# Attention scores as three fp32r products, with operand parts made by GpSimd, on one Trainium2 core

## The chip, the cores and the metric

The kernel runs as one program on one core of one Trainium2 chip. The metric is the device time of one execution in microseconds (us), told as a median of runs; lower is better.

## The reference

Two stages, all in float32. Attention with a bias that depends on position (batch 4, 8 heads, 576 positions, head size 64), then a feed-forward layer (2304 tokens, 512 to 2048 to 512) with a softplus between its two products.

```python
scores = q @ k.T / sqrt(D)                      # per batch and head, 576 x 576
x    = log1p(|i - j|) / log1p(max(i, 1))
bias = relu(x * w1 + b1) @ w2                   # one value per head, i, j
scores = scores + bias
attn = exp(scores - rowmax); attn /= rowsum + 1e-9
a    = attn @ v                                 # to (2304, 512)
out  = softplus(a @ moe_w_in) @ moe_w_out
```

## The kernel before

**The stages.** Up to about 62 us of the profiled span the bias is made, 16 rows at a time (36 steps), and written to DRAM (`e_d`). Then come the attention rounds. One round is one unit `n` (0 to 15: a pair of heads of one batch element). The rounds 2 to 14 are the steady ones; each takes 12.35 us. After round 16 comes the feed-forward layer, to the end at 673.7 us: per step twelve matmuls into `h` (L784) and twelve into `y` (L842), each already a sum of three fp32r products of a rounded part and the rest (`w_fin` at L751 and `x_prep` at L769 make the two parts with ScalarE and VectorE).

**One round.** A round is written by hand as a list of tokens (`ROUND`, L45). All engines take their instructions in the order of that list, each engine only its own, and no engine overtakes within itself. The loop at L969 hands each token to `emit` (L578):

- `S7/1` computes score tile 7 of the next unit, n+1, into PSUM bank 1 (`u_s`, L320, matmuls L347). The nine tiles of a unit are 128 rows by 576 columns; tile t is 128 queries of one head against all keys, tile 4 holds the last 64 queries of both heads. The head size of 64 fills half of TensorE's rows, so a tile is made as two halves of 288 columns, one on rows 0 to 63 and one on rows 64 to 127. These are plain fp32 matmuls, and the trace shows each of them as two instructions. There are four banks: 0, 1, 2 (the trace calls it `t`) and `o`.
- `A7` (VectorE, L365) adds the bias tile, takes the row minimum and puts the result to SBUF; `X7` (ScalarE, L383) is the exponential with its row sum.
- `L0` to `L4` (GpSimd, L400, `tail`) copy the last 64 columns of two tiles together.
- `T10/2` transposes three blocks of unit n into a bank (`turn`, L405), and `V10/a` or `V10/d` copies them to SBUF on ScalarE (a, L316) or VectorE (d, L318).
- `P0` to `P4` (L470) multiply by v; `P3` and `P4` of a unit stand in the next round. `O` (VectorE, L490) multiplies the output by the reciprocal row sums `rb`, and `Y` (L496 to L499) stores it with four DMAs to `x_d`.
- `I` (L508, L509) makes the reciprocals, `R` transposes them, `C` copies them to SBUF on ScalarE (L524) and stores them with a DMA that ScalarE issues (`r_d`, L525). `G` (L531, `queue`) loads them back as `rb` with three DMAs of SyncE, each spread over 64 partitions.
- `B0` to `B4` and `W` (`bits`, L665) turn 64-bit weight words into fp32: `B0` on ScalarE, `B1` on GpSimd (L676), `B2` (L679), `B3` (L685), `B4` (L690) on VectorE; `W` stores them (`w_d`, L711). `w` (L698), `v` (L292), `q` (L285), `k` (L279) and `b` (L306 to L311) are loads, all issued by SyncE; `q` and `k` in round n load unit n+3.

Unit n's scores are thus made in round n-1 and its transposes and products follow in round n. `SETS` (L52) says which bias tiles the tokens `b` of a round load. `ROUND14` (L70) is the last round with scores: its end holds `E` and `f0` to `f4`, which give the attention's memory to the feed-forward layer and issue its first loads. `ROUND15` and `ROUND16` carry the last products and the first two feed-forward steps.

Of the kernel before, what the change touches and what calls it, by code (L numbers as in the profile page):

```python
# [28 lines left out]
SH = S // 2  # L29
# [13 lines left out]


ROUND = """  # L45
T10/2 I T00/1 S2/2 S1/1 V10/a B0 S0/0 w T21/0 R/2 A1 C v P3 P4 q A0 V00/a S4/1 A2 B1 X1 k X0 O T40/1
S3/2 T12/o V21/a A4 V40/d X2 T01/2 Y T02/0 S8/o S5/1 V02/a V01/d b T41/0 T20/1 V12/a X4 T31/o L0 A3
G S7/0 S6/2 L4 A8 V20/a T22/1 T11/2 V41/a b V31/d T30/0 B2 A7 b X3 V11/a V22/a b P0 V30/d A5 A6 L1
X7 P1 X8 B3 X6 X5 L2 P2 T32/0 V32/d L3 B4 W
"""  # L50
STEADY = range(2, 17)
SETS = ((2, 4), (3, 8), (7, 5, 6), (1, 0))  # L52

ROUND0 = """
A6 A2 Z7 T10/1 A7 Z3 T20/0 V20/a T30/o A0 T00/2 ZA7 V00/d V30/a V10/a A1 A5 D6 Z8 X7 X2 ZX7 ZA3 X5
# [4 lines left out]

ROUND1 = """
I S4 T20/0 S3 A4 T11/1 A3 T00/2 S2 P3 X4 V00/d V20/a T02/0 V11/d T12/2 V02/a R/1 C P4 T41/0 S7
T22/1 S0 A2 O V12/a T01/o V41/a T10/0 V22/d L4 B0 T21/2 V01/a X3 A7 S1 V10/d P0 V21/a A0 T31/0
X2 T32/2 S5 X7 A1 P1 S6 V31/a V32/d X0 S8 B1 T30/1 X1 B2 L0 A5 T40/0 V30/a B3 L1 A8 V40/a X8 A6
X6 L3 P2 B4 X5 L2
"""

ROUND14 = """
T10/2 I T00/1 S2/2 S1/1 V10/a B0 S0/0 w T21/0 R/2 A1 C v P3 P4 q A0 V00/a S4/1 A2 B1 X1 k X0 O T40/1
S3/2 T12/o V21/a A4 V40/d X2 T01/2 Y T02/0 S8/o S5/1 V02/a V01/d b T41/0 T20/1 V12/a X4 T31/o L0 A3  # L70
G S7/0 S6/2 L4 A8 V20/a T22/1 T11/2 V41/a b V31/d T30/0 B2 A7 b X3 V11/a V22/a b P0 V30/d A5 A6 E f0
f1 f2 f3 f4 L1 X7 P1 X8 B3 X6 X5 L2 P2 T32/0 V32/d L3 B4
"""

ROUND15 = """
# [18 lines left out]
TAILS = ((0, 2), (1, 3), (5, 7), (6, 8), (4,))  # L94
CUT = (256, 320)
PV_LATE = 3
NAT = 4

RB_AFTER = 24
# [26 lines left out]
def tile_log_bias_attention__then__softplus_ffn(  # L126
# [144 lines left out]
    def emit_load(n, which="kq"):  # L271
# [4 lines left out]
        for nm in which:  # L276
# [43 lines left out]
    def u_s(n, t):  # L320

        pr, b = divmod(n, B)
        st_ = {}

        def pe(on=None):
            ssum[n] = sums[n % 3]
            if t == 4:
                prob[n, t] = pp.tile([128, S], F32, tag="p4", name="p4", bufs=2)
            elif (n, t) not in prob:
                i, two = next((i, two) for i, two in enumerate(TAILS) if t in two)  # L330
                pairs[n, i] = pp.tile([128, 2, S], F32, tag="p", name="p")
                for j, u in enumerate(two):
                    prob[n, u] = pairs[n, i][:, j]
            if on is None:
                b = s_use[0] % len(s_buf)
                s_use[0] += 1
            else:
                b = on
            assert b not in s_held
            s_held.add(b)  # L340
            ps = ps_o if b == "o" else s_buf[int(b)]
            st_["ps"], st_["s"] = ps[:, :, :SH], b
            for half in range(2):
                rows = slice(64 * half, 64 * half + 64)
                for hd in range(2) if t == 4 else (t // 5,):
                    at, c0, w = (64 * hd, 512, 64) if t == 4 else (0, 128 * (t % 5), 128)
                    nc.tensor.matmul(  # L347
                        ps[at:at + w, half, :SH],
                        lhsT=q_n[n][rows, hd, c0:c0 + w],
                        rhs=k_n[n][rows, hd],  # L350
                        start=True,
                        stop=True,
                        tile_position=(64 * half, at),
                    )

        def raw():
            p = prob[n, t].rearrange("p (a c) -> p a c", a=2)
            nc.scalar.activation(p, st_["ps"], AF.Copy)  # L358
            s_held.remove(st_.pop("s"))
            st_["ps"] = p  # L360

        def first():
            m = st.tile([128, 1], F32, tag="m", name="m", bufs=12)
            st_["m"] = m
            nc.vector.tensor_tensor_reduce(  # L365
                prob[n, t].rearrange("p (a c) -> p a c", a=2),
                st_["ps"],
                bias[pr, t].rearrange("p (a c) -> p a c", a=2),
                op0=ALU.add,
                op1=ALU.min,  # L370
                scale=-0.125,
                scalar=3.0e38,
                accum_out=m,
            )
            if "s" in st_:
                s_held.remove(st_["s"])
            if b == B - 1:
                bias.pop((pr, t))

        def second():  # L380
            done.add(("e", n, t))
            p = prob[n, t]
            nc.scalar.activation(  # L383
                p, p, AF.Exp, bias=st_["m"], scale=-1.0,
                accum_out=ssum[n][:, PLACE.index(t):PLACE.index(t) + 1],
            )

        return pe, first, second, raw
# [125 lines left out]
    def u_r(n):  # L514

        st_ = {}

        def pe(on=None):
            assert ("i", n) in done
            st_["ps"] = turn([ssum[n]], on)  # L520

        def first():
            r = st.tile([9, 128], F32, tag="r", name="r")
            nc.scalar.activation(r.rearrange("p (a c) -> p a c", a=2), st_["ps"][0:9, :, 0], AF.Copy)  # L524
            nc.scalar.dma_start(out=r_d[n], in_=r)  # L525

        def second():
            t = op_.tile([128, S], F32, tag="rb", name="rb")
            flat = r_d[n].rearrange("a b -> (a b)").rearrange("(o c) -> o c", o=1)
            for hd, lo, hi, c0 in ((0, 0, S, 0), (1, 256, S, S), (1, 0, 256, S + 320)):  # L530
                queue(n).dma_start(  # L531
                    out=t[64 * hd:64 * hd + 64, lo:hi],
                    in_=flat[:, c0:c0 + hi - lo].to_broadcast([64, hi - lo]),
                )
            rb[n] = t

        return pe, first, second
# [40 lines left out]
    def emit(n, tok):  # L578
# [14 lines left out]
        elif kind in ("Z", "ZA", "ZX"):  # L593
            stage(("s", n, *a), u_s, ("Z", "ZA", "ZX").index(kind))
        elif kind == "L":
            if n + 1 < N:
                tail(n + 1, *a)
        elif kind == "ZL":
            tail(n, *a)
        elif kind in ("T", "V"):  # L600
            stage(("t", n, *a), u_t, "TV".index(kind), *on)
        elif kind == "P":
            stage(("p", n - (a[0] >= PV_LATE), *a), u_pv, 0)
        elif kind == "I":
            inv(n)
        elif kind in ("R", "C"):
            stage(("r", n), u_r, "RC".index(kind), *on)
        elif kind == "O":
            if n:
                stage(("x", n - 1), u_x, 0)  # L610
                if n not in STEADY:
                    defer(8, lambda: stage(("x", n - 1), u_x, 1))
        elif kind == "B":
            i = min(n, N - 1) - 1
            if 0 <= i < len(pre):
                stage(("b", i), u_bits, *a)
                if a[0] == 4 and n not in STEADY:
                    defer(8, lambda: stage(("b", n - 1), u_bits, 5))
        elif kind in ("k", "q"):
            emit_load(n + 3, kind)  # L620
        elif kind == "v":
            emit_load_v(n + 2)
        elif kind == "w":
            pre_load(n)
        elif kind == "b":
            if tiles:
                emit_bias(*tiles.pop(0))
        elif kind == "G":
            units["r", n][2]()
        elif kind == "Y":  # L630
            stage(("x", n - 1), u_x, 1)
        elif kind == "W":
            i = n - 1 - (a[0] if a else 0)
            if 0 <= i < len(pre):
                stage(("b", i), u_bits, 5)
        elif kind == "D":
            for _ in range(a[0]):
                nc.tensor.transpose(ps_o[:, 0, SH:SH + 128], ident, ident)
        elif kind == "E":
            assert not s_held  # L640
# [250 lines left out]
    es_b.close()  # L891
    es_a = ctx.enter_context(ExitStack())
    vp = pool(es_a, "vp", 4)
    ptp = pool(es_a, "ptp", 5)
    op_ = pool(es_a, "op", 2)
    dec = pool(es_a, "dec", 2)
# [72 lines left out]
    for n in range(N + 1):  # L969
        tiles = [(n // B + 1 + (n % B == 3), t) for t in SETS[n % B]]  # L970
        if n < 3:
            tiles = [(1, t) for t in ((), range(5), range(5, 9))[n]]
        if n == 1:
            assert not s_held
            s_use[0] = 0
# [101 lines left out]
```

## Time and profile before

| what | value |
|---|---|
| median of the three runs shown | 675.04 us (673.45, 675.04, 809.87) |
| the profiled execution's own time | 675.52 us |
| its span (first to last instruction of the program) | 673.7 us |
| rounds 2 to 14 in that span | about 101.9 to 262 us, 13 rounds |
| TensorE (PE) busy | 643.7 us (96%) |
| VectorE (DVE) busy | 499.2 us (74%) |
| ScalarE (ACT) busy | 513.0 us (76%) |
| GpSimd (POOL) busy | 32.8 us (5%) |

Busy times are sums over the span; the names in the trace are PE for TensorE's matmuls, PEld for its weight loads, DVE, ACT, POOL, and SP for SyncE, whose work is to issue DMAs (SPq). A tile of the program stands as out<-in: `s<-kn,qn` is a score tile in one of the banks 0 and 1 (`t<-`, `o<-` in the other two), `o<-pt,vn` a product with v, `tl<-p` a tail copy.

### The profile page before, as it was taken

The page shows a single profiled execution, that of the slowest core. Times are in us where ns is not written, and L with a number is a line of the kernel's source. Part 1 is how long each engine was busy: PE and PEld are TensorE (multiplying, and loading weights), DVE is VectorE, ACT ScalarE, POOL GpSimd, SP SyncE. Part 2 cuts the span into 40 slices and gives each one's busy share as a digit, 9 for nine tenths or more (in the row PEclk, how much of TensorE's full clock was granted, in tenths as well). Part 3 has the DMA queues.
Part 4 walks back from the last instruction along what each step waited for, and adds up shares of the span by engine and source line. Part 5 has one row for each costly group of instructions (what it writes and reads, how often), then busy time and mean ns, then how long its engine had stood idle before and what let it go on. Part 6 is the DMA issues. An engine that isn't in the chain of part 4 may idle for free.

```text
span 673.7 us, 13202 instructions
## 1 busy us (share of the span) xinstructions
PE 643.7 (96%) x4807; PEld 479.0 (71%) x4807; DVE 499.2 (74%) x1084; ACT 513.0 (76%) x1059; POOL 32.8 (5%) x103
## 2 busy tenths in 40 slices
PE   5689789999999998999999999999999999999997
PEld 2124446766767665778888888888888888888886
DVE  6976659999998998787786965796774556556564
ACT  6798769999999998897785867785775665665654
POOL 0000101111111110000000000000000000000000
PEclk9879789999999999999999999999999999999999
DMA  5876938868879646551321204230200322202220
GB/s 150 310 239 226 344 118 277 280 226 291 282 242 283 212 150 209 163 191 44 142 78 48 102 9 151 74 121 33 78 17 0 113 76 106 82 0 87 70 95 32
DMA packets 51040, 96.84 MB, mean 144 GB/s; under 512 B 7440, under 2 KB 19104, under 8 KB 50976
## 3 DMA queue, kind: packets, MB, share of 16 engines
q1 hardware_dynamic: 50208, 95.34, 42.1%
q8 instruction: 38, 0.62, 0.4%
q10 hardware_dynamic: 768, 0.66, 0.3%
q14 instruction: 26, 0.21, 0.1%
HBM read 67.98 MB, written 28.01 MB: 142 GB/s over the span
## 4 chain that ended last, share of the span: by engine, by line
PE 88%; DMA 5%; ACT 3%; DVE 1%; SPq 1%; issue 1%; ACTq 0%; DVEq 0%
PE y L842 29%; PE h L784 29%; PE o L470 11%; PE s L347 6%; PE s L411 4%; PE acc L236 3%; PE t L347 3%; DMA e_d<-e 2%; PE t L411 1%; ACT e L257 1%; PE o L347 1%; PE o L411 1%; DMA dist<-in_c_dist_dram 1%; DMA a<-w_d 1%; DMA b<-e_d 1%
## 5 line engine op out<-in xcount | busy, mean ns | idle before, releaser
L784 PE MATMUL h<-x,wi 128*128 128x512 f32 (+1 forms) x960 | 211.7, 370 | 0.1
L842 PE MATMUL y<-wo,g 128*128 128x512 f32 x864 | 209.8, 391 | 0.0
L784 PEld LDWEIGHTS h<-x,wi 128*128 128x128 f32 x960 | 169.5, 189 | 33.2 <-DVE wi L757 0.5
L842 PEld LDWEIGHTS y<-wo,g 128*128 128x128 f32 x864 | 161.3, 188 | 33.6 <-DVE g L816 0.2
L807 DVE SCALAR_TENSOR_TENSOR u<-u,e 128x512 f32<-128x512 f32 (+1 forms) x80 | 51.0, 638 | 103.4 <-ACT l L804 103.1
L383 ACT ACTIVATE p<-p,m 128x576 f32<-128x576 f32 x144 | 110.4, 768 | 5.9 <-DVE m L365 2.4
L800 ACT ACTIVATE e<-h 128x512 f32<-128x512 f32 (+1 forms) x80 | 44.2, 553 | 77.3 <-PE h L784 77.2
L470 PE MATMUL o<-pt,vn 128*64 128x256 f32 (+3 forms) x640 | 83.5, 424 | 0.0
L365 DVE CUSTOM_DVE_ANT_0 p<-s,b 128x576 f32<-128x576 f32 x79 | 58.5, 753 | 10.0 <-ACT e L257 3.3
L814 ACT ACTIVATE g<-l 128x512 fp32r<-128x512 f32 (+1 forms) x80 | 46.8, 585 | 19.3 <-DVE l L811 9.8
L347 PE MATMUL s<-kn,qn 64*128 64x288 f32 (+1 forms) x416 | 59.2, 419 | 0.2 <-ACT p L358 0.2
L470 PEld LDWEIGHTS o<-pt,vn 128*64 128x64 f32 (+1 forms) x640 | 37.6, 138 | 27.8 <-issue 8.7
L816 DVE TENSOR_TENSOR g<-l,g 128x512 fp32r<-128x512 f32 (+1 forms) x80 | 50.4, 629 | 3.7 <-ACT g L814 3.7
L236 PE MATMUL acc<-m,coef 128*32 128x512 f32 (+17 forms) x352 | 38.3, 537 | 15.0 <-ACT e L257 7.7
L316 ACT ACTIVATE pt<-s 128x384 f32<-128x384 f32 (+1 forms) x94 | 44.7, 483 | 8.1 <-ACT r L524 4.6
L811 DVE TENSOR_TENSOR l<-l,u 128x512 f32<-128x512 f32 (+1 forms) x80 | 50.6, 632 | 0.0
L809 DVE SCALAR_TENSOR_TENSOR l<-h,l 128x512 f32<-128x512 f32 (+1 forms) x80 | 50.5, 631 | 0.0
L804 ACT ACTIVATE l<-u 128x512 f32<-128x512 f32 (+1 forms) x80 | 47.2, 589 | 2.9
L801 ACT ACTIVATE e<-e 128x512 f32<-128x512 f32 (+1 forms) x80 | 47.2, 590 | 2.5
L803 ACT ACTIVATE u<-e 128x512 f32<-128x512 f32 (+1 forms) x80 | 47.2, 590 | 2.6
L223 DVE TENSOR_SCALAR m<-lw,pb 128x576 f32<-128x576 f32 (+17 forms) x122 | 44.3, 443 | 1.0 <-PE acc L236 1.0
L411 PEld LDWEIGHTS s<-ident,p 64*128 64x128 f32 x672 | 32.4, 141 | 17.3 <-DVE m L365 7.4
(64 smaller groups left out, 677.3 us busy)
## 6 DMA issues: line engine op xcount, KB each, us to landing
e_d<-e SPq DMA_DIRECT2D x36, 295.5 KB, 3.4
qn<-in_q_dram SPq DMA_DIRECT2D x16, 576.0 KB, 6.2
b<-e_d SPq DMA_DIRECT2D x32, 288.0 KB, 3.4
r<-in_moe_w_in_dram SPq DMA_DIRECT2D x16, 512.0 KB, 3.4
r<-in_moe_w_out_dram SPq DMA_DIRECT2D x16, 512.0 KB, 4.6
xr<-x_d SPq DMA_DIRECT2D x28, 256.0 KB, 4.4
vn<-in_v_dram SPq DMA_DIRECT2D x16, 320.0 KB
kn<-in_k_dram SPq DMA_DIRECT2D x16, 288.0 KB, 6.3
```

Source lines behind the costliest of these rows:

```text
L236: nc.tensor.matmul(acc[32 * g:32 * g + 32, lo:hi], lhsT=coef.rearrange("p o h -> p (o h)"), rhs=hid[s, g][:, lo:hi], start=True, stop=True ...
L347: nc.tensor.matmul(ps[at:at + w, half, :SH], lhsT=q_n[n][rows, hd, c0:c0 + w], rhs=k_n[n][rows, hd], start=True, stop=True, tile_position= ...
L365: nc.vector.tensor_tensor_reduce(prob[n, t].rearrange("p (a c) -> p a c", a=2), st_["ps"], bias[pr, t].rearrange("p (a c) -> p a c", a=2), ...
L383: nc.scalar.activation(p, p, AF.Exp, bias=st_["m"], scale=-1.0, accum_out=ssum[n][:, PLACE.index(t):PLACE.index(t) + 1],)
L411: nc.tensor.transpose(ps[:, a, i], src[rows], ident[rows, 64 * a:64 * a + 64], tile_position=(64 * a, 0))
L470: nc.tensor.matmul(o[up, half, 0:w], lhsT=v_n[n][rows, jb, hd], rhs=pt[n, jb][rows, c0:c0 + w], start=(jb == 0), stop=(jb == 4), tile_posi ...
L784: nc.tensor.matmul(ps[:, :nb], lhsT=wi[f][:, a, 128 * c:128 * c + 128], rhs=xs[bi, c][:, x_, :nb], start=(i == 0), stop=(i == 11),)
L807: nc.vector.scalar_tensor_tensor(u, u, -1.0, e, op0=ALU.add, op1=ALU.subtract)
L809: nc.vector.scalar_tensor_tensor(l, ps, 0.0, l, op0=ALU.max, op1=ALU.add)
L811: nc.vector.tensor_tensor(l, l, u, op=ALU.subtract)
L816: nc.vector.tensor_tensor(g[:, 1], l, g[:, 0], op=ALU.subtract)
L842: nc.tensor.matmul(y, lhsT=g[:, a, 128 * ts:128 * ts + 128], rhs=wo[f][:, w_], start=(first and i == 0), stop=(last and i == 2),)
```

## The change

- From unit 3 on (`SPLIT = 3`) the eight score tiles other than tile 4 are made as three fp32r products: rounded q by rounded k, rest of q by rounded k, rounded q by rest of k, summed in PSUM. Per tile these are six matmuls of 288 columns (three for each half). Tile 4 stays fp32.
- The parts are made by GpSimd, six instructions for a unit (tokens `H0` to `H5`, two units ahead): `H0` copies k as fp32r (576 columns), `H1` subtracts to the rest, `H2` and `H4` copy the 512 used columns of q for either head, `H3` and `H5` subtract. They stand in `ROUND1` in one run and spread over `ROUND`. They live in a pool of their own, closed at `E`.
- `ROUND` and the first part of `ROUND14` have another order. VectorE's copies are V01, V11, V31, V30 in place of V40, V01, V31, V30, V32; ScalarE's are V10, V20, V00, V02, V12, V32, V41, V40, V22, V21 in place of V10, V00, V12, V21, V02, V20, V41, V11, V22. `R` and `C` stand behind `P4` and not ahead of `P3`; `q` and `k` stand behind `Y` and `C`, in the middle of the round.
- In the steady rounds the store of the reciprocals is issued by SyncE and not by ScalarE (`C/s`).
- `SETS` and the first bias tiles follow the new order.

```diff
--- before.py
+++ after.py
@@ -43,13 +43,13 @@
 
 
 ROUND = """
-T10/2 I T00/1 S2/2 S1/1 V10/a B0 S0/0 w T21/0 R/2 A1 C v P3 P4 q A0 V00/a S4/1 A2 B1 X1 k X0 O T40/1
-S3/2 T12/o V21/a A4 V40/d X2 T01/2 Y T02/0 S8/o S5/1 V02/a V01/d b T41/0 T20/1 V12/a X4 T31/o L0 A3
-G S7/0 S6/2 L4 A8 V20/a T22/1 T11/2 V41/a b V31/d T30/0 B2 A7 b X3 V11/a V22/a b P0 V30/d A5 A6 L1
-X7 P1 X8 B3 X6 X5 L2 P2 T32/0 V32/d L3 B4 W
+T01/0 B0 V01/d S7/1 T20/1 A7 H2 S1/2 w H0 T10/2 S3/0 T00/0 v I A3 V10/a H3 P3 A1 P4 O V20/a V00/a
+R/2 S6/1 H4 X7 Y T11/1 C/s X3 A6 S0/0 T02/0 V02/a B1 T31/o H1 q T12/2 S4/o V12/a V11/d A0 A4 k T41/1
+T32/2 S5/1 T40/0 X1 S2/0 b L1 V32/a B2 V41/a G V31/d S8/2 T22/2 V40/a B3 X0 b X4 T30/1 T21/0 A2 b
+V22/a P0 H5 A5 b V21/a X6 V30/d L4 X2 P1 A8 X5 L0 L2 X8 P2 B4 L3 W
 """
 STEADY = range(2, 17)
-SETS = ((2, 4), (3, 8), (7, 5, 6), (1, 0))
+SETS = ((1, 6), (0, 4), (2, 5, 8), (7, 3))
 
 ROUND0 = """
 A6 A2 Z7 T10/1 A7 Z3 T20/0 V20/a T30/o A0 T00/2 ZA7 V00/d V30/a V10/a A1 A5 D6 Z8 X7 X2 ZX7 ZA3 X5
@@ -60,16 +60,16 @@
 
 ROUND1 = """
 I S4 T20/0 S3 A4 T11/1 A3 T00/2 S2 P3 X4 V00/d V20/a T02/0 V11/d T12/2 V02/a R/1 C P4 T41/0 S7
-T22/1 S0 A2 O V12/a T01/o V41/a T10/0 V22/d L4 B0 T21/2 V01/a X3 A7 S1 V10/d P0 V21/a A0 T31/0
+T22/1 S0 A2 O H0 H1 H2 H3 H4 H5 V12/a T01/o V41/a T10/0 V22/d L4 B0 T21/2 V01/a X3 A7 S1 V10/d P0 V21/a A0 T31/0
 X2 T32/2 S5 X7 A1 P1 S6 V31/a V32/d X0 S8 B1 T30/1 X1 B2 L0 A5 T40/0 V30/a B3 L1 A8 V40/a X8 A6
 X6 L3 P2 B4 X5 L2
 """
 
 ROUND14 = """
-T10/2 I T00/1 S2/2 S1/1 V10/a B0 S0/0 w T21/0 R/2 A1 C v P3 P4 q A0 V00/a S4/1 A2 B1 X1 k X0 O T40/1
...
+T01/0 B0 V01/d S7/1 T20/1 A7 S1/2 w T10/2 S3/0 T00/0 v I A3 V10/a P3 A1 P4 O V20/a V00/a R/2 S6/1 X7
+Y T11/1 C/s X3 A6 S0/0 T02/0 V02/a B1 T31/o q T12/2 S4/o V12/a V11/d A0 A4 k T41/1 T32/2 S5/1 T40/0
...
+X6 V30/d L4 X2 P1 A8 E f0 f1 f2 f3 f4 X5 L0 L2 X8 P2 B4 L3
 """
@@ -94,6 +94,7 @@
 TAILS = ((0, 2), (1, 3), (5, 7), (6, 8), (4,))
 CUT = (256, 320)
 PV_LATE = 3
+SPLIT = 3
 NAT = 4
 
 RB_AFTER = 24
@@ -285,6 +286,28 @@
                 nc.sync.dma_start(out=t, in_=q[b, pr].rearrange("a d h s -> (a d) h s"))
                 q_n[n] = t
 
+    q_h, q_l, k_h, k_l = {}, {}, {}, {}
+
+    def split(n, i):
+
+        if n >= N:
+            return
+        hd = (i - 2) // 2
+        if i == 0:
+            k_h[n] = sp.tile([128, 2, SH], F32R, tag="kh", name="kh")
+            nc.gpsimd.tensor_copy(k_h[n], k_n[n])
+        elif i == 1:
+            k_l[n] = sp.tile([128, 2, SH], F32R, tag="kl", name="kl")
+            nc.gpsimd.tensor_tensor(k_l[n], k_n[n], k_h[n], op=ALU.subtract)
+        elif i % 2 == 0:
+            if n not in q_h:
+                q_h[n] = sp.tile([128, 2, 512], F32R, tag="qh", name="qh")
+            nc.gpsimd.tensor_copy(q_h[n][:, hd], q_n[n][:, hd, :512])
+        else:
+            if n not in q_l:
+                q_l[n] = sp.tile([128, 2, 512], F32R, tag="ql", name="ql")
+            nc.gpsimd.tensor_tensor(q_l[n][:, hd], q_n[n][:, hd, :512], q_h[n][:, hd], op=ALU.subtract)
+
     def emit_load_v(n):
         if n >= N:
             return
@@ -340,6 +363,20 @@
             s_held.add(b)
             ps = ps_o if b == "o" else s_buf[int(b)]
             st_["ps"], st_["s"] = ps[:, :, :SH], b
+            if n >= SPLIT and t != 4:
+                hd, c0 = t // 5, 128 * (t % 5)
+                for i, (a, c) in enumerate(((q_h[n], k_h[n]), (q_l[n], k_h[n]), (q_h[n], k_l[n]))):
+                    for half in range(2):
+                        rows = slice(64 * half, 64 * half + 64)
+                        nc.tensor.matmul(
+                            ps[:, half, :SH],
+                            lhsT=a[rows, hd, c0:c0 + 128],
+                            rhs=c[rows, hd],
+                            start=(i == 0),
+                            stop=(i == 2),
+                            tile_position=(64 * half, 0),
+                        )
+                return
             for half in range(2):
                 rows = slice(64 * half, 64 * half + 64)
                 for hd in range(2) if t == 4 else (t // 5,):
@@ -519,10 +556,10 @@
             assert ("i", n) in done
             st_["ps"] = turn([ssum[n]], on)
 
-        def first():
+        def first(on="a"):
             r = st.tile([9, 128], F32, tag="r", name="r")
             nc.scalar.activation(r.rearrange("p (a c) -> p a c", a=2), st_["ps"][0:9, :, 0], AF.Copy)
-            nc.scalar.dma_start(out=r_d[n], in_=r)
+            (nc.sync if on == "s" else nc.scalar).dma_start(out=r_d[n], in_=r)
 
         def second():
             t = op_.tile([128, S], F32, tag="rb", name="rb")
@@ -625,6 +662,8 @@
         elif kind == "b":
             if tiles:
                 emit_bias(*tiles.pop(0))
+        elif kind == "H":
+            split(n + 2, *a)
         elif kind == "G":
             units["r", n][2]()
         elif kind == "Y":
@@ -638,6 +677,7 @@
                 nc.tensor.transpose(ps_o[:, 0, SH:SH + 128], ident, ident)
         elif kind == "E":
             assert not s_held
+            es_h.close()
             es_s.close()
             open_ffn()
         elif kind == "F":
@@ -891,6 +931,8 @@
     es_b.close()
     es_a = ctx.enter_context(ExitStack())
     vp = pool(es_a, "vp", 4)
+    es_h = ctx.enter_context(ExitStack())
+    sp = pool(es_h, "sp", 2, "right")
     ptp = pool(es_a, "ptp", 5)
     op_ = pool(es_a, "op", 2)
     dec = pool(es_a, "dec", 2)
@@ -969,7 +1011,7 @@
     for n in range(N + 1):
         tiles = [(n // B + 1 + (n % B == 3), t) for t in SETS[n % B]]
         if n < 3:
-            tiles = [(1, t) for t in ((), range(5), range(5, 9))[n]]
+            tiles = [(1, t) for t in ((), (7, 3, 1, 6, 0), (4, 2, 5, 8))[n]]
         if n == 1:
             assert not s_held
             s_use[0] = 0
```

## Rows read from the trace of the kernel before

**Rows 1.** The page: chain that ended last, shares of the span by engine.
```profile
PE 88%; DMA 5%; ACT 3%; DVE 1%; SPq 1%; issue 1%; ACTq 0%; DVEq 0%
```

**Rows 2.** Busy times by window, five steady rounds: the first, and the mean.
```profile
138.00:150.35 12.35, 12.35 (x166) 8.59 (x164) 11.32 (x31) 11.73 (x30) 2.03 (x6) 1.00 0.70 238
...
sum 61.75, PE 61.75 PEld 42.95 DVE 56.62 ACT 58.66 POOL 10.18; mean PE 12.35 PEld 8.59 DVE 11.32 ACT 11.73 POOL 2.04
```

**Rows 3.** Chain that ended last, 113.26 to 199.69 us (seven rounds): shares by line.
```profile
by line: PE o L470 39.5%; PE s L347 20.4%; PE s L411 15.3%; PE t L347 12.7%; PE t L411 5.0%; PE o L347 4.4%; PE o L411 3.0%
```

**Rows 4.** The same chain by time, round from 162.6 us: start, us, what.
```profile
165.68 0.48 PE s L347 x8
...
167.53 0.54 PE o L347 x4
168.06 0.48 PE s L347 x4
```

**Rows 5.** Timeline of the weight loads, first two and all four of one tile.
```profile
166.21 0.20 PEld L347 LDWEIGHTS t<-kn,qn 64*128 64x128 f32 x2
...
166.21 0.31 PEld L347 LDWEIGHTS t<-kn,qn 64*128 64x128 f32 x4
```

**Rows 6.** Chain that ended last, feed-forward layer: twelve fp32r matmuls of 512 columns.
```profile
304.25 2.80 PE h L784 x12
```

**Rows 7.** Timeline of ScalarE, a steady round (idle time before it in brackets).
```profile
152.17 0.49 ACT L316 ACTIVATE pt<-s 128x384 f32<-128x384 f32 x1 [0.35 <-ACT r L524]
152.55 0.77 ACT L383 ACTIVATE p<-p,m 128x576 f32<-128x576 f32 x1
...
153.31 0.76 ACT L383 ACTIVATE p<-p,m 128x576 f32<-128x576 f32 x1
```

**Rows 8.** Groups of instructions by form: GpSimd's two, and VectorE's clamp.
```profile
L400 POOL COPY tl<-p 128x128 f32<-128x128 f32 x65 | 18.5, 295 | 126.2 <-ACT p L383 109.5 <-issue 16.2 <-POOL tl L400 0.5
L676 POOL TENSOR_SCALAR a<-a 128x512 f32<-128x512 f32 x13 | 8.0, 613 | 6.9 <-ACT a L673 6.9
...
L676 DVE TENSOR_SCALAR a<-a 128x512 f32<-128x512 f32 x17 | 7.1, 420 | 0.0
```

**Rows 9.** Groups of VectorE, 100 to 260 us: `B3`, the mean of 13.
```profile
L685 DVE SCALAR_TENSOR_TENSOR b<-r,b 128x512 int32<-128x512 int32 x13 | 9.0, 689 | 0.0
```

**Rows 10.** Timeline of GpSimd and of VectorE where two instructions lie beside each other.
```profile
97.08 0.29 POOL L400 COPY tl<-p 128x128 f32<-128x128 f32 x1 [7.78 <-issue]
...
97.16 0.75 DVE L685 SCALAR_TENSOR_TENSOR b<-r,b 128x512 int32<-128x512 int32 x1
```

**Rows 11.** Timeline of VectorE and SyncE, one round: output multiply, stores, reciprocal loads.
```profile
153.38 0.42 DVE L490 TENSOR_TENSOR x<-o,rb 128x256 f32<-128x256 f32 x1 [0.42 <-PE o L470]
...
154.59 0.47 SPq L497 DMA_DIRECT2D x_d<-x  x1
...
157.19 2.03 SPq L531 DMA_DIRECT2D rb<-r_d  x2
```

**Rows 12.** SyncE's waits, 100 to 250 us: us in total, times, longest us.
```profile
SPq L531 <- DMA qn<-in_q_dram: 14.9, 11, 3.1
```

**Rows 13.** DMA issues, 100 to 260 us: KB each, median us from issue to landing.
```profile
w_d<-a SPq DMA_DIRECT2D x13, 256.0 KB, 2.5
...
x_d<-x SPq DMA_DIRECT2D x13, 80.0 KB, 5.4
...
rb<-r_d SPq DMA_DIRECT2D x13, 64.0 KB, 3.5
```

**Rows 14.** Landing times of the second output store (L497), 100 to 250 us.
```profile
DMA to landing us min/median/max: 5.4/6.6/7.8
```

**Rows 15.** Chain that ended last, behind the last scores: start, us, what.
```profile
252.15 0.77 DVE x L490 x2
...
256.26 0.54 SPq L531
...
265.86 0.43 DVE x L490 x2
```

More of the change, by code (lines that the diff above doesn't have):

```diff
@@ L68 @@
 ROUND14 = """
-T10/2 I T00/1 S2/2 S1/1 V10/a B0 S0/0 w T21/0 R/2 A1 C v P3 P4 q A0 V00/a S4/1 A2 B1 X1 k X0 O T40/1
-S3/2 T12/o V21/a A4 V40/d X2 T01/2 Y T02/0 S8/o S5/1 V02/a V01/d b T41/0 T20/1 V12/a X4 T31/o L0 A3
-G S7/0 S6/2 L4 A8 V20/a T22/1 T11/2 V41/a b V31/d T30/0 B2 A7 b X3 V11/a V22/a b P0 V30/d A5 A6 E f0
-f1 f2 f3 f4 L1 X7 P1 X8 B3 X6 X5 L2 P2 T32/0 V32/d L3 B4
+T01/0 B0 V01/d S7/1 T20/1 A7 S1/2 w T10/2 S3/0 T00/0 v I A3 V10/a P3 A1 P4 O V20/a V00/a R/2 S6/1 X7
+Y T11/1 C/s X3 A6 S0/0 T02/0 V02/a B1 T31/o q T12/2 S4/o V12/a V11/d A0 A4 k T41/1 T32/2 S5/1 T40/0
+X1 S2/0 b L1 V32/a B2 V41/a G V31/d S8/2 T22/2 V40/a B3 X0 b X4 T30/1 T21/0 A2 b V22/a P0 A5 b V21/a
+X6 V30/d L4 X2 P1 A8 E f0 f1 f2 f3 f4 X5 L0 L2 X8 P2 B4 L3
 """
```

## The prediction

> **What bounds the kernel now.** I read the chain of waits first: 88% of the span is TensorE's [rows 1]. The change acts on the 13 steady rounds, 2 to 14, so I read windows there next. In each round of 12.35 us TensorE has no idle time at all, with the clock granted in full (1.00, the level of 2.4 GHz), ScalarE is busy for 11.73, VectorE for 11.32, GpSimd for 2.04 [rows 2]. The reader should see two things in that. TensorE's work alone sets a steady round, so work taken from it comes back as time. And the two engines behind it leave only 0.6 and 1.0 us, so it can't come back for long. ScalarE's need is less than its busy time, as neighbours overlap: by starts, a copy takes 0.38 us (152.17 to 152.55) and an exponential with its sum 0.76 (152.55 to 153.31), and 0.35 idle stands behind the DMA that it issues [rows 7]. Nine of each make 10.3; the copy of the weight words and that of the reciprocals, some 0.9, make 11.1.
>
> **The score tiles.** In seven rounds (86.43 us) the chain spends 20.4 + 12.7 + 4.4 = 37.5% on score tiles [rows 3], 32.4 us, 4.63 a round. Tile 4, which stays, takes 0.48 [rows 4]; the other eight take 4.15, 0.519 each. By pieces it is 0.48 behind another score tile and 0.54 behind a transpose [rows 4]: there the first weights are not yet loaded, 0.06 more.
>
> Now the new tile. Two halves of 288 columns run beside each other: four fp32 instructions fill 0.48 us, so a pair lasts 0.242, two clocks a column plus 2 ns. For fp32r the only rows are the feed-forward layer's: 2.80/12 = 0.233 us for 512 columns [rows 6], one clock a column (0.213) plus 20 ns. A pair of fp32r products of 288 columns thus takes 0.120 plus 2 ns (as between the fp32 passes) to 0.120 plus 20 ns: 0.122 to 0.140. I take 0.131, the feed-forward row scaled by columns, as the nearest. Three make 0.393; seven of the eight tiles stand behind a transpose in the new order (all but S8), so 0.06 x 7/8 comes on top: 0.445. Saved: 0.519 - 0.445 = 0.074 a tile, 0.59 a round (0.37 by 0.140, 0.80 by 0.122).
>
> A load of 128 columns of weights has to fit beside each short product. At a tile's start the first two loads end 0.20 us after their start and the next two 0.11 later [rows 5]: one takes some 0.11 us for both halves, just under 0.120. The Trainium skill (TensorE: Matmul & The Clock Gate, LDWEIGHTS) gives columns over 1.2 GHz, 107 ns, and this row agrees. The same page (What overlaps and what doesn't) lets a load overlap a running matmul only where their rows differ; by that, each product would show its load, 3 x (0.120 + 0.107) = 0.68 a tile. The feed-forward rows, on all rows of the array, hide such loads in 0.233, so the trace speaks against it for long matmuls; for 0.120 nothing shows it. That is rival D.
>
> **GpSimd's parts.** Six instructions a round. Its copy of 128 columns takes 0.295 us, its clamp of 512 takes 0.613 [rows 8]: 0.83 ns a column. Three copies (576, 512, 512) cost 0.67 + 2 x 0.61 = 1.9. For two inputs there is no row of GpSimd. From below it is the one-input time, 0.61; VectorE's two-input instruction takes 0.69 [rows 9], and GpSimd takes 0.613 where VectorE takes 0.420 for the same clamp [rows 8], 1.46 times: 1.0 us for 512; from above I take twice that. With 1.0 the three subtractions make 3.1 (1.9 to 6.3). GpSimd's round: 2.0 + 1.9 + 3.1 = 7.0, at most 10.2, under the round. I cost it at nothing; the cover is GpSimd's idle 10 us. What waits in its queue is `B1`, and behind that `B2` on VectorE: `H2` waits for q, loaded now in mid-round, and if q lands over 3 us into the next round VectorE stands still at `B2`.
>
> Do the engines hurt each other? The one place with GpSimd's copy beside VectorE's two-input `B3`, 0.2 us of overlap [rows 10]: `B3` took 0.75 for 0.689 [rows 9], the copy 0.29 as ever. So 0.06 per 0.2 of overlap; `B3` and `B4` wholly covered would lose 0.4 us a round, nothing from below. VectorE has no tile-4 copy of 256 columns any more (0.3 less), and hides this. The Trainium skill (SBUF — State Buffer, Who interferes with whom) says that the second to issue blocks fully; the trace shows a slowing instead. By the page VectorE would stand for a whole subtraction, 1 us, as often as they meet.
>
> **ScalarE and SyncE.** ScalarE loses the idle 0.35 and gets one copy of 256 columns, 0.3: need 11.1 + 0.3 = 11.4. That lies below the new round (11.8), with 0.4 to spare. SyncE gets one issue of 0.3 us. The waits behind it count for more: the store now stands behind the four output stores, and the loads `G` need its landing.
>
> **The sum.** Round: 12.35 - 0.59 = 11.76. With three engines within 0.4 to 0.8 us of that, in one fixed order, I give 0.1 back for waits of TensorE (0 to all): 0.49 x 13 = 6.4 us. **The end of round 14** gives some back. From the output multiply at 252.15 to the next one at 265.86 the chain runs over SyncE: stores, `rb` loads right behind them at 256.26, then the feed-forward loads [rows 15]. There the reciprocals' store had been issued early by ScalarE. Now it comes between: 0.3 us to issue, then its landing, for which the nearest row is 2.5 us [rows 13]. All behind it is late by up to 2.8, 0 if other waits hide it. I take 2.0. GpSimd's run in round 1 costs nothing: what needs it comes a round later. The other bias order (`SETS`) loads the same 36 tiles, into the same 18 buffers, well ahead of their use; I cost it at nothing, and were a tile late, `A` would wait for it by name. Total: -6.4 + 2.0 = -4.4. On the profiled execution (675.52, of which 673.7 is span and 1.8 lies around it, unchanged) that is 671.1; it stands 0.5 above the median 675.04, so the prediction for a median is 670.6.
>
> **The rivals.**
>
> *A, the full gain.* Products at 0.122 and no waits, no loss at the end: 0.80 x 13 = 10.4, 664.6. For it: TensorE had no gap in any steady round [rows 2]. Against: ScalarE needs 11.4, and the round would be 11.55.
>
> *B, another engine or queue holds the round.* ScalarE, VectorE or GpSimd's late q take back most: round at 12.2 or more, at most 2 us saved, 2 lost at the end: 675. For it: the 0.6 us of ScalarE [rows 2]. Against: 0.35 of its time goes.
>
> *C, slower: the loop of the reciprocals.* SyncE's rows show that the second `rb` load waits for the landing of q's load [rows 12], the eighth DMA before it in program order. In the new order the eighth before it is the second output store. That closes a loop over rounds: output multiply to that store's issue, 153.38 to 154.59, 1.2 us; its landing, 5.4 to 7.8 [rows 13, 14]; two `rb` issues, 1.0 (two with a wait span 2.03) [rows 11]; landing of the last, 3.5 [rows 13]; then the next round's output multiply, at which VectorE waits and behind it the score tiles. Sum 11.1 to 13.5. It decides once the store lands later than 11.8 - 5.7 = 6.1 us. At 7.8 each round takes 13.5, which is 1.15 longer: 675 + 15 + 2 = 692. Against: q's big load no longer stands ahead of the store, so it should land sooner.
>
> *D, slower: the short products don't stream.* If a pair of fp32r products takes as long as an fp32 pass (0.242; weights not hidden, or the halves one behind the other), a tile takes 3 x 0.242 + 0.05 = 0.78, 0.26 more, 2.1 a round, 27 in all: 704 with the end. Break-even is 0.156 a product.
>
> **How the numbers follow.** Forecast 0.52, its own range 666 to 674 (0.37 to 0.80 a round less waits; the end 0 to 2.8). A 0.14, B 0.15, C 0.12, D 0.07. A measurement of this kernel can tell about 2%, 13.5 us. Faster by more (below 661.5) needs over 1.04 a round, beyond A's end: 0.05. Slower by more (above 688.5): D and two thirds of C, 0.15. Within 2%: 0.80. The range for 8 in 10 leaves out D, half of C and the end of A: 662 to 686.
>
> **What would show it.** Right: in the steady rounds a product pair every 0.13 us, a score tile of 0.42 to 0.47, a round near 11.9, GpSimd at about 7, TensorE idle under 0.2 a round; the `rb` loads of round 14 two to three us behind the last output store. A wrong step: score tiles over 0.52 (D); the output multiply waiting for `rb` (C); ScalarE without gaps or VectorE waiting for `B1` (B); subtractions over 2 us.

## The result and the profile after

The changed kernel takes 678.86 us (median of 4 runs, 678.42 to 680.06) against 674.27 before: 1.0075 times the time, 95% interval 1.0052 to 1.0098. It is slower by 4.6 us where 4.4 us less were forecast. One of the four runs before, of 809.87 us, lies in a slow state and is left out of the ratio. The profiled execution has a span of 676.6 us, 2.9 more than before.

The page, chain that ended last: TensorE's share falls from 88% to 79%, and VectorE's rises from 1% to 7% [rows 1].

```profile
PE 79%; DVE 7%; DMA 6%; ACT 3%; SPq 2%; issue 2%; POOL 0%; ACTq 0%; DVEq 0%; POOLq 0%
```

Busy times by window, one steady round: its length, the busy time of PE, PEld, VectorE, ScalarE and GpSimd with the number of instructions, the granted clock, the DMA share, GB/s. To be set beside [rows 2]: the round is 12.75 and not 12.35 us, TensorE has gaps again (12.20 busy), VectorE went from 11.32 to 12.02 although a copy was taken from it, GpSimd from 2.0 to 7.8.

```profile
137.10:149.85 12.75, 12.20 (x184) 8.92 (x182) 12.02 (x29) 11.86 (x32) 7.84 (x13) 1.00 0.77 240
```

The chain by time in a steady round (start, us, what, number of instructions). To be set beside [rows 4]: a score tile behind a transpose is 0.46 where it was 0.54. But the chain now leaves TensorE in mid-round and runs through VectorE, with 1.44 us in one instruction, `B2` (L719, which was L679), before P0 to P2.

```profile
151.91 0.46 PE s L371 x6
...
155.30 1.44 DVE b L719
156.74 0.48 DVE pt L341
...
157.26 3.13 PE o L507 x24
```

What is wrong with `B2` shows when the timelines of the two engines are laid side by side. GpSimd:

```profile
155.17 1.29 POOL L309 TENSOR_TENSOR ql<-qn,qh 128x512 fp32r<-128x512 f32 x1
```

VectorE:

```profile
155.21 1.53 DVE L719 TENSOR_SCALAR b<-a 128x512 int32<-128x512 int32 x1
```

and TensorE, with the idle time before P0 in brackets:

```profile
157.26 3.13 PE L507 MATMUL o<-pt,vn 128*64 128x256 f32 x24 [0.55 <-DVE pt L341]
```

`H5`, GpSimd's subtraction, starts at 155.17. `B2` starts 0.04 us later and ends at 156.74, 0.28 behind `H5`'s end at 156.46. Before, the whole instruction took 0.417, so all but 0.14 us of it lies behind `H5`. Behind it waits the copy V31/d, and behind that TensorE. This happens in each of the twelve rounds in which parts are made (1.40 to 1.54 us), and only to this instruction of VectorE. Groups of VectorE by form, 100 to 260 us (busy us, mean ns); the mean of 1433 has in it the 0.42 of round 14, where `H5` is missing. The reduction that takes one input out of PSUM (L402) is at 752 with GpSimd busy beside it in many of its runs; before, with GpSimd mostly idle, the same group (L365 there) had 753.

```profile
L402 DVE CUSTOM_DVE_ANT_0 p<-s,b 128x576 f32<-128x576 f32 x76 | 56.2, 752 | 3.9 <-PE s L448 2.1
...
L719 DVE TENSOR_SCALAR b<-a 128x512 int32<-128x512 int32 x13 | 18.6, 1433 | 0.0
```

Groups of GpSimd, 60 to 270 us: the parts cost 1.28 and 1.42 a subtraction, 0.61 and 0.66 a copy, 5.9 us a round.

```profile
L309 POOL TENSOR_TENSOR ql<-qn,qh 128x512 fp32r<-128x512 f32 x26 | 33.3, 1281 | 0.2
...
L305 POOL CAST qh<-qn 128x512 fp32r<-128x512 f32 x26 | 15.8, 610 | 0.0
```

### The profile page after: what moved, and what is told of

Its sections match the earlier page's. It is cut to its first block, busy times and chain, and to the rows that moved or that the text cites. A ratio compares the mean times of both kernels' runs of the same rounds, so it can differ in the third digit from the quotient of the medians.

```text
span 676.6 us, 13698 instructions
## 1 busy us (share of the span) xinstructions
PE 640.7 (95%) x5015; PEld 483.9 (72%) x5015; DVE 507.0 (75%) x1071; ACT 514.6 (76%) x1072; POOL 108.6 (16%) x181
## 4 chain that ended last, share of the span: by engine, by line
PE 79%; DVE 7%; DMA 6%; ACT 3%; SPq 2%; issue 2%; POOL 0%; ACTq 0%; DVEq 0%; POOLq 0%
PE y L882 29%; PE h L824 29%; PE o L507 10%; PE acc L237 4%; DVE p L402 2%; PE s L371 2%; DVE b L719 2%; PE s L448 2%; DMA rb<-r_d 1%; DMA e_d<-e 1%; DVE pt L341 1%; PE s L384 1%; ACT e L258 1%; PE t L448 1%; DMA w_d<-a 1%
## 5 line engine op out<-in xcount | busy, mean ns | idle before, releaser
L402 DVE CUSTOM_DVE_ANT_0 p<-s,b 128x576 f32<-128x576 f32 x92 | 68.2, 752 | 12.3 <-ACT e L258 3.4
L437 POOL COPY tl<-p 128x128 f32<-128x128 f32 x80 | 26.0, 327 | 153.3 <-ACT p L420 150.5
L448 PEld LDWEIGHTS s<-ident,p 64*128 64x128 f32 x672 | 33.0, 141 | 12.5 <-DVE m L402 5.9
```

Source lines behind the costliest of these rows:

```text
L402: nc.vector.tensor_tensor_reduce(prob[n, t].rearrange("p (a c) -> p a c", a=2), st_["ps"], bias[pr, t].rearrange("p (a c) -> p a c", a=2), ...
L448: nc.tensor.transpose(ps[:, a, i], src[rows], ident[rows, 64 * a:64 * a + 64], tile_position=(64 * a, 0))
```

## The experiments

In the diffs, minus is the changed kernel and plus the experiment; they are shortened, and where an edit changes `ROUND14` in the same way, only `ROUND` is shown. Ratios are against the kernel before, with 95% intervals.

### One: B2 and B3 five instructions later

```diff
-... X1 S2/0 b L1 V32/a B2 V41/a G V31/d S8/2 T22/2 V40/a B3 X0 b X4 T30/1 T21/0 A2 b
-V22/a P0 H5 A5 b ...
+... X1 S2/0 b L1 V32/a V41/a G V31/d S8/2 T22/2 V40/a X0 b X4 T30/1 T21/0 A2 b
+V22/a P0 H5 A5 B2 B3 b ...
```

> B2 and B3 (VectorE's mask and shift of the weight words) stand five VectorE instructions later in the steady rounds, behind A5, so that B2 no longer starts while GpSimd subtracts in H5. Nothing else changes. Theory 1 (the two-engine collision): in the changed kernel B2 takes 1.43 us beside H5 where it took 0.42 before, and V31/d and P0 wait behind it; with the collision gone B2 is back near 0.42, VectorE's busy time falls from 12.02 to about 11.0 a round, the round from 12.75 to 11.8 to 12.0, and the kernel, over 12 such rounds, to about 667 to 671. Theory 2 (the order and the loop over the reciprocals' store hold the round): B2 is short but the wait moves to the output multiply or to S4, the round stays at 12.4 or more and the kernel at 675 to 679. Theory 3 (GpSimd slows all of VectorE): the other instructions of VectorE get longer and the round stays.

Measured: 678.38 us, ratio 1.0042 (1.0019 to 1.0066). The round is 12.6. Groups of VectorE, 100 to 260 us:

```profile
L719 DVE TENSOR_SCALAR b<-a 128x512 int32<-128x512 int32 x13 | 5.5, 422 | 0.0
```

Timeline of VectorE, the wait of `A2` in brackets:

```profile
158.47 0.76 DVE L402 CUSTOM_DVE_ANT_0 p<-s,b 128x576 f32<-128x576 f32 x1 [1.10 <-PE s L448]
```

`B2` is whole again, as theory 1 wanted, and the round is hardly better, as theory 2 wanted. The second row says why. `A2` now stands right behind V31/d and waits 1.10 us for a transpose (L448): in the list T21/0 writes `A2`'s bank ahead of it, and by this row `A2` waits for the newest write to its bank and not for its own scores. In the changed list `B2` and `B3` filled that time. So this run shows that the collision can be removed, but not what it costs.

### Two: B2 with two inputs in the same place

```diff
-                nc.vector.tensor_scalar(b, a, 3, 0x3FFFFFFF, shift_left, and)
+                nc.vector.scalar_tensor_tensor(b, a, 3, mask, shift_left, and)   # mask: constant tile
```

> B2 stays in its place beside H5, but is made with two SBUF inputs (the mask comes from a small constant tile and not as an immediate), so it is the same kind of instruction as B3, 0.69 us alone. If H5 holds off any VectorE instruction that reads SBUF twice or in its fast form, B2 again lasts until H5 ends, about 1.4 us, and the kernel stays at 678 to 680. If only the fast one-input form is held off and a two-input form is merely slowed (as the one overlap in the trace of before showed, 0.75 for 0.69), B2 takes 0.8 to 1.0, the round 12.2 to 12.4, and the kernel 672 to 675.

Measured: 681.45 us, ratio 1.0107 (1.0067 to 1.0146); the profile is of the longest of its four runs, 687.21 us, and its round is 13.0. Groups of VectorE, 100 to 260 us:

```profile
L721 DVE SCALAR_TENSOR_TENSOR b<-a,mask 128x512 int32<-128x512 int32 x13 | 22.2, 1707 | 0.0
```

Timeline of GpSimd, then of VectorE:

```profile
162.63 1.29 POOL L309 TENSOR_TENSOR ql<-qn,qh 128x512 fp32r<-128x512 f32 x1
```

```profile
162.68 1.79 DVE L721 SCALAR_TENSOR_TENSOR b<-a,mask 128x512 int32<-128x512 int32 x1
```

The two-input form is held off just the same: it ends 0.55 us behind `H5`, and takes 1.79 where this form takes 0.69 alone [rows 9]. "Merely slowed", my reading of the overlap in [rows 10], is wrong, and those rows already show it: there `B3` ends 0.54 behind the copy (97.91 and 97.37), as here. The copy of 0.29 us was only too short for the wait to be seen as one.

### Three: no parts made

```diff
-        hd = (i - 2) // 2
-        if i == 0:
-            ...
+        k_h[n], k_l[n], q_h[n], q_l[n] = parts        # four constant tiles, filled once
```

> The parts of q and k are not made: all three products read four constant tiles filled once, so GpSimd has none of the six instructions per round. The order, the fp32r products and SyncE's store stay. This shows what the products and the order are worth without GpSimd's work. Theory 1: B2 is 0.42, the round 11.7 to 11.9, the kernel 666 to 669. Theory 2: the round stays over 12.3, the kernel at 674 or more. If the round falls under e1's, the difference is what GpSimd's other instructions still cost.

Measured: 672.16 us, ratio 0.9939 (0.9908 to 0.9970). Busy times by window, one steady round:

```profile
148.60:160.72 12.12, 12.12 (x183) 8.93 (x180) 11.13 (x30) 11.74 (x31) 2.08 (x6) 1.00 0.87 283
```

Without GpSimd's work the round is 12.12 with no gap on TensorE: the making of the parts costs the changed kernel 0.63 a round. But 12.12 is not the 11.8 that I had worked out for TensorE. The scores of this kernel are not those of q and k, since its parts are constants.

### Four: the store on ScalarE again

```diff
-R/2 S6/1 H4 X7 Y T11/1 C/s X3 ...
+R/2 S6/1 H4 X7 Y T11/1 C X3 ...
```

> The store of the reciprocals is issued by ScalarE again, at the same place of the order; all else as changed. Theory 1: ScalarE has 0.35 us more idle time a round but VectorE sets it, so the round stays at 12.7; the end of round 14 gets 0.5 to 2 us shorter, since SyncE's loads no longer stand behind the store's landing: the kernel 677 to 679. Theory 2: with the store ahead of the output stores the loop over the rounds is open and the round falls to 12.3 or less, the kernel to 674 or less.

Measured: 672.21 us, ratio 0.9947 (0.9923 to 0.9972). Busy times by window:

```profile
148.60:160.72 12.12, 12.12 (x184) 8.94 (x183) 11.51 (x30) 11.69 (x31) 8.05 (x13) 1.00 0.88 270
```

By the number alone this is theory 2: the store moved and the round fell to 12.12. The timelines say otherwise. GpSimd:

```profile
153.99 1.51 POOL L309 TENSOR_TENSOR ql<-qn,qh 128x512 fp32r<-128x512 f32 x1
```

VectorE:

```profile
153.94 0.42 DVE L719 TENSOR_SCALAR b<-a 128x512 int32<-128x512 int32 x1
...
154.75 1.31 DVE L725 SCALAR_TENSOR_TENSOR b<-r,b 128x512 int32<-128x512 int32 x1
```

Here `B2` starts 0.05 us ahead of `H5`, not 0.04 behind. Now `H5` is held (1.51 for 1.28) and `B2` is whole. Then `B3`, with two inputs, runs into `H5` and ends 0.56 behind it, 1.31 for 0.69: a loss of 0.6 and not 1.0, and behind P0's copy in the list, so VectorE takes it without holding TensorE. I read the store's part as this: the DMA issue makes ScalarE's exponentials later, `L1` waits for one of them, and `H5` stands behind `L1`. `L1`'s copy comes 5.14 us after P3 here (153.75 and 148.61), 5.03 in the changed kernel (154.92 and 149.89).

### Five: H5 behind L4, store on SyncE

```diff
-V22/a P0 H5 A5 b V21/a X6 V30/d L4 X2 ...
+V22/a P0 A5 b V21/a X6 V30/d L4 H5 X2 ...
```

> One token moves: GpSimd's H5 stands behind L4 and not behind L1, so GpSimd starts it some 3 us later, where VectorE only copies and reduces out of PSUM. VectorE's and SyncE's lists stay as changed, the store of the reciprocals on SyncE included. Theory 1 (the collision of H5 with B2 is the whole loss of a steady round): B2 is back to 0.42, the round from 12.75 to 12.12, as with the store on ScalarE and with no parts made, and the kernel to 670 to 673. Theory 2 (the store on SyncE holds the round): B2 is short and the round stays over 12.4, the kernel over 675.

Measured: 671.14 us, ratio 0.9965 (0.9942 to 0.9988). Groups of VectorE, 100 to 250 us, and two starts of P3 in the chain, 12.12 apart:

```profile
L719 DVE TENSOR_SCALAR b<-a 128x512 int32<-128x512 int32 x12 | 5.1, 423 | 0.0
```

```profile
147.84 1.82 PE o L507 x16
...
159.96 1.82 PE o L507 x16
```

This is theory 1 as expected: SyncE keeps the store, one GpSimd token moves, and the round is 12.12.

### Six: B2 one instruction earlier

```diff
-... V12/a V11/d A0 A4 k T41/1 ... L1 V32/a B2 V41/a ...
+... V12/a V11/d A0 B2 A4 k T41/1 ... L1 V32/a V41/a ...
```

> The changed kernel with one token moved: B2 stands one VectorE instruction earlier, ahead of A4, so that it starts 0.6 us before GpSimd can start H5; H5, the store on SyncE and all else stay. Theory 1, in the form that the one that starts first keeps the other out: B2 takes 0.42 to 0.6 (the end of H1 may still reach into it), the round 12.12 to 12.2, the kernel 670 to 673, as with H5 moved. If the time of day of the two is not the cause, B2 or B3 is long again and the round over 12.5.

Measured: 671.19 us, ratio 0.9949 (0.9925 to 0.9972); most rounds 12.12. Groups of VectorE, 100 to 250 us:

```profile
L725 DVE SCALAR_TENSOR_TENSOR b<-r,b 128x512 int32<-128x512 int32 x13 | 12.2, 938 | 0.0
...
L719 DVE TENSOR_SCALAR b<-a 128x512 int32<-128x512 int32 x13 | 5.7, 437 | 0.0
```

A start 0.6 us earlier is enough; part of the loss moves to `B3` (0.94 for 0.69), where it is hidden.

### Seven: the order alone

```diff
-SPLIT = 3
+SPLIT = 99          # all tiles fp32, and no parts made
```

> The new order and SyncE's store alone: all score tiles stay fp32 and GpSimd makes no parts. Theory 4: TensorE has no gap and needs 0.3 us more than before, the round 12.6 to 12.75, the kernel 679 to 683. If the new order costs TensorE nothing, the round is 12.35 and the kernel 674 to 677 (with up to 2 us for the end of round 14).

Measured: 680.07 us, ratio 1.0085 (1.0060 to 1.0110). The chain by time:

```profile
138.24 1.82 PE o L507 x16
...
151.05 1.82 PE o L507 x16
...
153.08 0.54 PE s L384 x4
...
154.89 0.65 PE o L384 x8
155.54 0.33 PE s L448 x6
```

TensorE has no gap, and its round is 12.81, 0.46 more than in the old order with the same matmuls. Three more tiles stand behind a transpose at 0.54 (seven of eight, four before), 0.17 in all; I had that in the tile's price. Tile 4, whose matmuls use quarters of the array, takes 0.65 between transposes where it took 0.48 behind P4 [rows 4]. The rest is one change more from quarters to transposes; P4, too, ends in matmuls on quarters. In the old order P4, tile 4 and four transposes follow each other, and those four take 0.27 where four take 0.12 elsewhere, 0.15 more. In the new order this is paid twice: by the two transposes of the sums behind P4 (0.21, where they took 0.06 ahead of P3) and by the six behind tile 4 (0.33 for 0.18). The chain of the kernel before:

```profile
163.80 0.06 PE t L411 x2
...
166.16 0.27 PE s L411 x4
```

The chain of the fourth experiment shows the new order with the fp32r tiles:

```profile
150.43 0.21 PE t L448 x2
150.64 0.46 PE s L371 x6
...
152.29 0.65 PE o L384 x8
152.94 0.33 PE s L448 x6
...
153.91 0.12 PE s L448 x4
...
154.48 0.40 PE t L371 x6
```

### Eight: the old order with the products

```diff
-(ROUND, ROUND14, SETS and the store of the changed kernel)
+(those of the kernel before, with the parts made here:)
+... A2 B1 H2 H0 H3 H4 X1 ... T31/o L0 H1 A3 ... A5 A6 L1 H5 X7 ...
```

> The products and GpSimd's parts in the old order: ROUND, ROUND14, SETS and the store on ScalarE are those of before, with H2, H0, H3, H4 behind B1, H1 behind L0 and H5 behind L1, where VectorE has no instruction of the weight words. Tile 4 stands behind P4. Theories 1 and 4 together: TensorE needs 12.35 - 0.57 = 11.8 a round; if it sets the round, the kernel is at 666 to 669, the best so far; if ScalarE or VectorE holds at 12.0 to 12.2, 670 to 673. If GpSimd meets B2 or B3 after all, that instruction lasts over 1 us and the round is 12.4 or more.

Measured: 669.53 us, ratio 0.9929 (0.9905 to 0.9954), faster than both kernels; the fastest of the twelve. The chain by time:

```profile
138.43 1.82 PE o L507 x16
...
150.49 1.82 PE o L507 x16
152.31 0.48 PE s L384 x8
...
162.29 0.25 PE t L448 x2
```

`B2` and `B3` are short and tile 4 is back at 0.48, yet the round is 12.06 and not 11.8. Of the 0.25 missing, 0.19 stand at the transposes of the sums (0.25; they were 0.06) and 0.07 at P0 to P2 (3.13 for 3.06), with no other change over 0.03 in TensorE's pieces. I read these as waits that TensorE's modelled ends hide. For the sums the engine is VectorE. Its reciprocals end at 162.12:

```profile
161.91 0.21 DVE L546 RECIPROCAL ss<-ss 128x9 f32<-128x9 f32 x1
```

TensorE's transposes of them start at 162.27, 0.15 later, and so in each of the nine rounds from 138 to 235 us. In the kernel before they start 0.37 to 0.38 behind the reciprocals. What P0 to P2 wait for was not settled.

### Nine to twelve: tile 4 behind P4 in the new order

```diff
-        ... P3 A1 P4 O V20/a V00/a R/2 S6/1 H4 X7 Y T11/1 C/s X3 A6 ... S4/o ... A0 A4
+nine:   ... P4 S4/1 O V20/a V00/a R/2 H4 X7 Y T11/1 C X3 A4 ... S6/o ... A0 A6
+ten:    ... P4 O V20/a V00/a S4/1 R/2 H4 X7 Y T11/1 C X3 A4 ... S6/o ... A0 A6   (H5 behind L4)
+eleven: ... P4 R/2 O V20/a V00/a S4/1 H4 X7 Y T11/1 C/s X3 A4 ... S6/o ... A0 A6  (H5 behind L4)
```

> The kernel with the store on ScalarE (round 12.12, TensorE without a gap), and score tiles 4 and 6 change places: tile 4, whose matmuls use quarters of the array, stands right behind P4, where the old order had it, and tile 6 goes to bank o between the transposes. Theory 4 (the new order costs TensorE 0.3 us a round by where tile 4 stands: 0.65 for tile 4 where it took 0.48, and 0.33 for the transposes behind it where they take 0.18): tile 4 is back to 0.48, the round 11.8 to 11.9 if no other engine holds it, the kernel 666 to 669. If ScalarE (11.4 by its starts) or VectorE holds the round, TensorE shows gaps and the round is 11.9 to 12.1. Against theory 4: the 0.17 and 0.15 go with any tile at that place, and the round stays at 12.12.

Nine measured 693.49 us, ratio 1.0285 (1.0255 to 1.0316). Timeline of ScalarE, the copy V20/a:

```profile
156.95 0.87 ACT L339 ACTIVATE pt<-s 128x384 f32<-128x384 f32 x2 [1.82 <-issue]
```

V20/a waits 1.82 us, until tile 4 is done: tile 4 is written to the same bank and stands ahead of it in the list, as T21/0 stood ahead of `A2` in the first experiment.

> The new order with both mends (store of the reciprocals on ScalarE, H5 behind L4), and tile 4 in place of tile 6 behind P4 as in the kernel with that swap before, but V20/a and V00/a now stand ahead of S4/1 in the list, so that V20/a does not wait for tile 4 as the newest write to its bank. Theory 4: tile 4 takes 0.48 again, the transposes where it stood 0.18, and the round falls from 12.12 to 11.8 to 11.9; kernel 666 to 668. If waits of TensorE that its modelled ends hide take the gain, the round is 11.95 to 12.1 and the kernel 668 to 671. Against theory 4: round 12.12 or more.

Ten measured 677.88 us, ratio 1.0040 (1.0015 to 1.0066), round 12.54. The chain by time:

```profile
150.22 0.48 PE s L384 x8
150.70 0.23 PE t L448 x2
...
150.95 0.28 ACT r L561
...
151.25 0.30 ACTq L562
...
151.60 0.87 ACT p L420 x2
```

Tile 4 is 0.48 again, 0.17 less than between transposes, but the sums come behind it (0.23), and ScalarE's exponentials wait behind the copy and the issue for the sums.

> As the swap of tiles 4 and 6 with V20/a and V00/a ahead, but R (the transposes of the sums) stands between P4 and tile 4, so that ScalarE's copy C and the exponentials behind it no longer wait for tile 4, and the store is on SyncE, so that ScalarE has not its 0.3 us either. H5 stays behind L4. Theory 4: tile 4 0.48 and the transposes at its old place 0.18, ScalarE no longer holds TensorE, the round 11.8 to 12.0, the kernel 665 to 669. If ScalarE or VectorE hold the round with any place of tile 4, it is 12.1 to 12.5 and the kernel 670 to 677; then TensorE's 0.3 us of dear places can't be had back in this order.

Eleven measured 674.15 us, ratio 0.9984 (0.9962 to 1.0006), round 12.31. The chain by time:

```profile
152.10 0.21 PE t L447 x2
152.31 0.65 PE s L383 x8
```

With the sums between, tile 4 is at 0.65 again. It is the transpose ahead of it that counts, not the place in the round. So in this order the 0.3 us could be had only at the price of waits that cost more; of it only the 0.17 at tile 4 can be read, in ten.

> The new order with the store on ScalarE and H5 behind L4; tile 4 stays between the transposes. Each of the two edits alone gave a round of 12.12 with TensorE without a gap. If TensorE's own work sets it, both together give 12.12 again and the kernel is at 669 to 672; a round under 12.05 would say that VectorE or ScalarE still held TensorE in either.

Twelve, the changed kernel with the store on ScalarE and `H5` behind `L4`, measured 671.04 us, ratio 0.9958 (0.9935 to 0.9981), and 12.12 in most rounds: the two mends don't add up, since either alone leaves TensorE without a gap (12.12 of 12.12).

## Why the prediction was wrong

**What bounds the kernel: right.** TensorE set the round, and sets it again in this order wherever neither the collision nor a wait for a bank holds it (12.12 of 12.12 in three, four, five, six and twelve).

**The price of a tile: right.** 0.445 was predicted. The eight tiles of the fourth experiment's chain take 0.46, 0.45, 0.46, 0.45, 0.40, 0.46, 0.45 and 0.45, 3.58 in all, 0.448 each. The price of an old tile was taken a little high: by the pieces of one round the eight take 4.09 (four of 0.54, four of 0.48 to 0.49), not the 4.15 that I had from the shares of the chain. So 0.51 a round is saved on them, and 0.59 was predicted. Rival D is excluded: the weights hide behind short products. The rule of the Trainium skill weighed there (TensorE: Matmul & The Clock Gate, What overlaps and what doesn't), by which a tile would be 0.68, disagrees with these rows.

**The first step that failed: "`B3` and `B4` wholly covered would lose 0.4 us a round", which VectorE "hides", and with it "I cost it at nothing".** I took the 0.06 us that `B3` lost beside a copy of 0.29 us as a slowing in proportion to the overlap, scaled it, and left out `B2`. In fact the first to start holds the other off almost to its own end: 1.1 us on `B2` (1.53 for 0.42) in each round in which GpSimd is 0.04 us ahead, in front of the copy that P0 waits for. It makes the round 12.75 in place of 12.12, 0.63 for each of the twelve rounds with parts, 7.6 us, and so the sign of the result. Four runs show it from four sides: no parts (12.12), `H5` moved (12.12), `B2` moved (12.12), two inputs in the same place (13.0). How the two engines shut each other out no run shows. The rule that I had set aside (the Trainium skill, SBUF — State Buffer, Who interferes with whom), by which the second to issue blocks fully, agrees with these runs.

**The second: the sum counted the new order as free on TensorE.** "Tile 4, which stays, takes 0.48" was a price for its old place. Beyond the eight tiles' own price the order costs 0.28 a round: 12.12 against 12.35 - 0.51 = 11.84. Tile 4 behind a transpose carries 0.17 of it, the second change from quarters to transposes up to 0.15. Without any collision the change would thus be worth 0.23 a round, 3 us. The runs with parts made in which the collision doesn't hold TensorE (four, five, six, twelve) lie 2.4 to 3.6 us below before by their ratios.

**The third: "I take 2.0" for the end of round 14.** From P3 of round 14 to the first feed-forward matmul the kernel before takes 23.11 us (250.28 to 273.39), the fourth experiment (store on ScalarE) 22.82 and the fifth (store on SyncE) 22.83: the store's place costs nothing there. The chain of the fifth:

```profile
244.79 1.82 PE o L507 x16
...
267.62 5.68 PE h L824 x24
```

In the changed kernel the same stretch is 24.26, with the same list for round 14 as in the fifth:

```profile
252.24 1.82 PE o L507 x16
...
265.34 3.42 PE o L507 x16
...
276.50 5.69 PE h L824 x24
```

The 1.4 us more come from TensorE's clock. P3 and P4 of round 15 take 3.42 us, where these sixteen matmuls take 1.82 in round 14. The granted clock is 0.50 there, the level of 1.2 GHz:

```profile
265.30:268.70 3.40, 3.40 (x20) 1.08 (x18) 1.84 (x3) 1.53 (x3) 0.00 (x0) 0.50 0.92 343
```

In the fifth experiment the clock at this place is 1.00 (257.80 to 259.60 us). In both TensorE had waited 1.4 us for VectorE's reciprocals just before. Seven of the fourteen profiles have a mean clock of 0.50 to 0.60 at this place and 23.9 to 24.4 us for the stretch, twelve with its store on ScalarE among them; the other seven have 1.00 there, and but for nine they take 22.4 to 23.3 us. What decides between the two no run shows. Nor was it traced why round 2 begins some 3 us earlier in the changed kernel's profile (98.91) than before (102.12), which the 2.9 us in the spans contains.

**GpSimd's price: in the bounds.** 1.28 for a subtraction (1.0 taken, 0.61 to 2.0), 7.8 for its round (7.0). **ScalarE and SyncE: no limit at 12.12.** With the store on SyncE the rounds run at 12.12 and the loop of rival C does not bind. Whether ScalarE would allow 11.8 no run shows. Rival B, "another engine or queue holds the round", is what happened, but by a lock of two engines and not by a need, and it made the rounds longer than before (12.75 and 12.35), where B still had up to 2 us saved in them.

## What to carry to other kernels

Work given to an idle GpSimd was free here only where its instructions did not meet an instruction of VectorE that takes all its inputs out of SBUF: list what VectorE reads, and look at who starts first, because 0.1 us there decided over 1.1 us on `B2` in every round. When an order is rewritten, price each instruction of the bounding engine anew by what stands ahead of it, also those that are not changed. And in two runs a reader of a bank waited for the newest write that stood ahead of it in the list (1.10 and 1.82 us), so a tile moved up past a reader holds that reader.

## What the runs showed of the hardware that I had not expected

GpSimd and VectorE shut each other out for nearly a whole instruction, in both directions: `B2` 1.53 for 0.42 and, with two inputs, 1.79 for 0.69 when `H5` was first; `H5` 1.51 for 1.28 when `B2` was first. The one held off ends 0.14 us less than its own length behind the first (0.28 of 0.42, 0.55 of 0.69). VectorE's instructions with one input out of PSUM don't feel it (752 ns beside GpSimd as without). On TensorE a tile in quarters of the array costs 0.17 us more behind transposes than behind other quarters (0.65 and 0.48, the latter behind P4, which ends in quarters), and transposes behind it 0.15 more than behind themselves (0.33 and 0.18). TensorE's granted clock fell to 0.50 for one stretch behind a wait of 1.4 us in some runs, and stayed at 1.00 behind the same wait in others.
